# K cache transposed from rows of four keys, and probabilities kept in the V order, in a two-problem attention kernel

## The chip, the cores and the metric

The kernel runs on one core of a Trainium2 chip. The metric is device time in microseconds of one launch, the median of three runs.

## What is computed

Two independent attention problems, A and B, have the same shapes: a batch of 16, 144 queries, a model width of 448, 16 heads of width 256, and a cache of 512 keys and values for each head. All arrays are bf16.

```python
q = (x @ wq).reshape(B, Sq, H, Dh).transpose(0, 2, 1, 3)
scores = jnp.einsum("bhqd,bhkd->bhqk", q, k_cache) * (Dh ** -0.5)
p = _softmax(scores, axis=-1)
o = jnp.einsum("bhqk,bhkd->bhqd", p, v_cache)
return o.transpose(0, 2, 1, 3).reshape(B, Sq, H * Dh) @ wo
```

The two results are joined along the last axis. The softmax and the product with V do not depend on the order of the keys, as long as both use the same order.

## The kernel before

A unit is one head of one batch of one problem; there are 512 units, numbered U. Eight units form a super-group SG (64 of them), four units a group G.

For each unit the program does the following. `t_q` (L338) computes q transposed, 2 x 128 rows by 144 columns, in eight matmuls. `t_evac_q` writes it, scaled, to `qt_sb`. The 144 queries are then handled in two parts. The first 112 go unit by unit: `t_sa` (L471) makes the scores 112 x 512 in two matmuls of 512 columns, with the transposed K as the moving operand. `t_max` (L482) takes the row maximum, `t_exp` (L493) the exponential, `t_recip` and `t_norm` (L503, L511) the normalisation in `pa_sb`. `t_ta` (L524) transposes the 112 x 512 probabilities in four TensorE transposes, in which the probabilities are the loaded weights and the identity is the moving operand. `t_evac_pta` (L534) copies them to `pt_sb`. `t_pv` (L557) multiplies with V in eight matmuls of 144 columns. The last 32 queries of four units are stacked to 128 rows: `t_sb` (L374) computes the scores of eight units in 16 matmuls, four of them side by side in the array; `t_max_b`, `t_exp_b` (L397), `t_recip_b`, `t_norm_b` follow. Their transposition to `pbt_sb` is done by a DMA (`t_ptb_dma`, L425), or, in 18 super-groups at the start and the middle, by TensorE (`t_tb`, L437). `t_op_piece` (L595) does the output projection of 128-row chunks, two matmuls at a time, between the units.

K reaches SBUF through `t_load_k` (L306), one DMA transpose for each super-group: 8 x 512 keys by 256 (2 MB) from DRAM. The source is a matrix of 4096 rows of 512 bytes, and the destination, in `kt_sb`, has two runs of 4096 elements on each partition. The compiled transpose moves it in blocks of 16 rows by 128 columns. `kt_sb` has two slots (NK = 2), so the load of super-group n + 2 waits until the last `t_sa` of super-group n is done. V comes through `t_load_v` (L316), 1 MB for a group, where partition p holds the keys 4p to 4p + 3 in one run of 2 KB. So the transposes of P have to deliver the keys 4p + c for each c from 0 to 3. In the first part `t_ta` reads every fourth column of `pa_sb` for that (the keys lie there in natural order). In the second part `t_exp_b` writes its result in the order c, p while it reads the scores from PSUM with a step of four.

All loads, stores and DMA transposes are issued by SyncE in one order fixed beforehand (`dma_plan`, from L649). From super-group 8 on it repeats every 16 units: for two super-groups n and n + 1 there are a load of x where one is due, pb(n), k(n + 2), pb(n + 1), k(n + 3), and four loads of V. The order of the instructions on the other engines is written out in the loop from L740. `_Sched.add` derives the waits from reads and writes.

Of the kernel before, what the change touches and what calls it, by code (L numbers as in the profile page):

```python
# [5 lines left out]
BF16 = mybir.dt.bfloat16  # L6
F32 = mybir.dt.float32
AF = mybir.ActivationFunctionType
# [114 lines left out]
def bass_concat_heads__mha_block_cached__gqa_block_cached__near_ridge_kernel(  # L123
# [19 lines left out]
    Bn, SQ, D = A_x.shape  # L143
    H, SK, DH = A_k_cache.shape[1], A_k_cache.shape[2], A_k_cache.shape[3]
    assert (SQ, D, SK, DH) == (144, 448, 512, 256), (SQ, D, SK, DH)
    assert H % 4 == 0
    QA, QB = 112, 32
# [18 lines left out]
    NK, NV, NXG = 2, 5, 2  # L166
# [5 lines left out]
    NQT, NPA, NPB, NPT, NST, NSTB, NOST = 12, 14, 2, 8, 4, 2, 3  # L172
    NPBT = 1
    RS = 4
    RC = RS * 128
    OP_DELAY = 2
    assert NT % 8 == 0
# [4 lines left out]
    with contextlib.ExitStack() as es:  # L182
        def sb(name, shape, dt):
            return es.enter_context(nc.sbuf_tensor(name, shape, dt))

        def ps(name, shape, dt):
            return es.enter_context(nc.psum_tensor(name, shape, dt))

        wq_sb = sb("wq_sb", [128, 4, H * DH], BF16)
        wo_sb = sb("wo_sb", [128, NWO, D], BF16)  # L190
        ring = sb("ring", [128, NWO, RC], BF16)
        kt_sb = sb("kt_sb", [128, 2, NK * 8 * SK], BF16)
        v_sb = sb("v_sb", [128, NV, 4, 4 * DH], BF16)
        xt_sb = sb("xt_sb", [128, NXG, 4, XB * SQ], BF16)
        qt_sb = sb("qt_sb", [128, NQT, 2, SQ], BF16)
        pa_sb = sb("pa_sb", [128, NPA, SK], BF16)
        pb_sb = sb("pb_sb", [128, NPB, 2, SK], BF16)
# [6 lines left out]
        sa_ps = [ps("sa_ps%d" % i, [128, 512], F32) for i in range(2)]  # L204
        sb_ps = [ps("sb_ps%d" % i, [128, 512], F32) for i in range(2)]
# [94 lines left out]
        def t_load_k(SG):  # L300
            pr, r0 = divmod(8 * SG, NU)
            sl = SG % NK
            src = ks[pr].rearrange("b h k d -> (b h k) d")[r0 * SK:(r0 + 8) * SK, :]

            def e(q):
                return q.dma_start_transpose(kt_sb[:, :, sl * 8 * SK:(sl + 1) * 8 * SK], src).then_inc(  # L306
                    sems["kt%d" % sl], 16)
            S.add(SP, e, writes=[(("kt", sl), SG)], dma_sem="kt%d" % sl, name="k%d" % SG)

# [48 lines left out]
        def t_warm(k):  # L358
            def e(t):
                ins = None  # L360
                for _ in range(N_WARM[k]):
# [2 lines left out]
            S.add(PE, e, reads=[("ident", 0), ("warm", 0)], writes=[(("sbb", 1), ("w", k))], banks=["sb1"],  # L364
                  name="W%d" % k)

        def t_sb(SG):
            def e(t):
                ins = None
                for dc in range(2):  # L370
                    for jj in range(8):
                        U = 8 * SG + jj
                        j = jj % 4
                        ins = t.matmul(sb_ps[jj // 4][32 * j:32 * j + 32, :], lhsT=qt_sb[:, U % NQT, dc, QA:SQ],  # L374
                                       rhs=kt_sb[:, dc, (U % (8 * NK)) * SK:(U % (8 * NK) + 1) * SK], start=(dc == 0),
                                       stop=(dc == 1), tile_position=(0, 32 * j))
                return ins
            S.add(PE, e, reads=[(("qt", (8 * SG + jj) % NQT), 8 * SG + jj) for jj in range(8)] +
                  [(("kt", SG % NK), SG)],
                  writes=[(("sbb", 0), ("s", 2 * SG)), (("sbb", 1), ("s", 2 * SG + 1))], banks=["sb0", "sb1"],  # L380
                  name="SB%d" % SG)
# [10 lines left out]
        def t_exp_b(G):  # L392
            sl = G % NSTB
            psl = (G // 2) % NPB

            def e(a):
                return a.activation(pb_sb[:, psl, G % 2, :], sb_ps[G % 2][:, :].rearrange("q (p c) -> q c p", c=4), AF.Exp,  # L397
                                    bias=stat[:, NEGB + sl:NEGB + sl + 1], scale=1.0,
                                    accum_out=stat[:, RSUMB + sl:RSUMB + sl + 1])
            S.add(ACT, e, reads=[(("sbb", G % 2), ("s", G)), (("negb", sl), G)],  # L400
                  writes=[(("pb", psl, G % 2), (G, 0)), (("rsumb", sl), G)], banks=["sb%d" % (G % 2)], name="exb%d" % G)
# [60 lines left out]
        def t_sa(U):  # L462
            SG = U // 8
            ksl = SG % NK
            bank = U % 2
            ko = (U % (8 * NK)) * SK

            def e(t):
                ins = None
                for dc in range(2):  # L470
                    ins = t.matmul(sa_ps[bank][0:QA, :], lhsT=qt_sb[:, U % NQT, dc, 0:QA],  # L471
                                   rhs=kt_sb[:, dc, ko:ko + SK], start=(dc == 0), stop=(dc == 1))
                return ins
            S.add(PE, e, reads=[(("qt", U % NQT), U), (("kt", ksl), SG)], writes=[(("sap", bank), ("s", U))],
                  banks=["sa%d" % bank], name="SA%d" % U)
# [40 lines left out]
        def t_ta(U):  # L516
            psl = U % NPA
            bank = ta_bank[U]

            def e(t):  # L520
                src = pa_sb[0:QA, psl, :].rearrange("q (p c) -> q c p", c=4)
                ins = None
                for c in range(4):
                    ins = t.transpose(pta_ps[bank][:, c * 128:c * 128 + QA], src[:, c, :], ident[0:QA, 0:QA])  # L524
                return ins
            S.add(PE, e, reads=[(("pa", psl), (U, 1)), ("ident", 0)], writes=[(("sap", bank), ("t", U))],
                  banks=["sa%d" % bank], name="TA%d" % U)
# [11 lines left out]
        def ring_cols(pr, b):  # L539
            g0 = pr * RP + b * SQ  # L540
            return g0, g0 % RC

        def chunks_of_batch(pr, b):
            g0 = pr * RP + b * SQ
            return list(range(g0 // 128, (g0 + SQ - 1) // 128 + 1))
# [18 lines left out]
        def t_evac_ot(U):  # L564
            pr, b, h = unit(U)
            g0, c0 = ring_cols(pr, b)
            n1 = min(SQ, RC - c0)
            ob = U % 2

            def e(a):  # L570
                src = ot_ps[ob][:, 0:2 * SQ].rearrange("p (c q) -> p c q", c=2)
                ins = a.activation(ring[:, 2 * h:2 * h + 2, c0:c0 + n1], src[:, :, 0:n1], AF.Copy)  # L572
                if n1 < SQ:
                    ins = a.activation(ring[:, 2 * h:2 * h + 2, 0:SQ - n1], src[:, :, n1:SQ], AF.Copy)
                return ins
            S.add(ACT, e, reads=[(("otp", ob), U)], writes=[(("ring", r % RS, h), r) for r in chunks_of_batch(pr, b)],
                  banks=["ot%d" % ob], name="eot%d" % U)

        def chunk_rows(r):
            pr, rl = divmod(r, NCH)  # L580
            row0 = rl * 128
            m = min(128, Bn * SQ - row0)
            return pr, row0, m

        def t_op_piece(r, cs, bank):
            pr, row0, m = chunk_rows(r)
            col0 = (r % RS) * 128
            acc = op_ps if bank == "op" else qp_ps
# [11 lines left out]
            for hh in sorted(set(c // 2 for c in cs)):  # L600
                assert len(S.res[("ring", r % RS, hh)].writers) == nb, (r, hh, nb)
                rd.append((("ring", r % RS, hh), r))
            S.add(PE, e, reads=rd + [(("wo", wg), pr) for wg in sorted(set(c // WOG for c in cs))],
# [84 lines left out]
        for n in range(RAMP, NSG, 2):  # L688
            t = 8 * n
# [41 lines left out]
        def pop_items(bank, i, n):  # L731
            q = fifo[bank]
            r = q[0][0]
            cs = []
            while q and len(cs) < n and q[0][0] == r and q[0][2] <= i:
                cs.append(q.pop(0)[1])
            return r, cs

        i = s_min
        while True:  # L740
# [3 lines left out]
            n = max(k for k in range(-1, NSG) if k < 0 or sb_slot[k] <= i)  # L744
# [21 lines left out]
            for u in sas:  # L766
                if 8 <= u and u + 8 < NT:
                    t_q(u + 8)
                    t_evac_q(u + 8)
                if u % 8 == 0:  # L770
                    t_sb(u // 8)
                t_sa(u)
                if u < 8:
                    t_q(u + 8)
                    t_evac_q(u + 8)
                t_max(u)
                t_exp(u)
                last_sa = u
# [43 lines left out]
            for bank in ("op", "qp"):  # L822
                while fifo[bank] and fifo[bank][0][2] <= i and credit >= 1 and (bank == "qp" or i >= op_hold):
                    r, cs = pop_items(bank, i, OPP)
# [67 lines left out]
```

## Time and profile before

| | |
|---|---|
| median of three runs | 1217.22 us (1211.76 to 1221.06) |
| profiled execution | 1215.54 us |
| its span, first to last instruction | 1213.8 us |
| granted TensorE clock, mean | 0.992 |
| busy: TensorE, VectorE, ScalarE, GpSimd | 96%, 61%, 62%, 60% |
| DMA packets on SyncE's queue | 679424, 304.05 MB |

A busy time is the union of the intervals of an engine's instructions; a matmul's interval includes its way through the array, which overlaps the next one. Two matmuls that follow each other closely are therefore better read by the distance between their starts. PE is TensorE's matmul, PEld its weight load, which runs beside the matmuls.

### The profile page before, as it was taken

The numbers are of one execution on the slowest core, as the hardware profiler recorded it, in microseconds if no ns is written. First come the engines' busy times: TensorE is split into PE (matmuls) and PEld (weight loads), VectorE is DVE, ScalarE is ACT, GpSimd is POOL, SyncE is SP. The second block draws the span as 40 slices with busy tenths as digits, with TensorE's granted clock in tenths as the row PEclk, the third lists the DMA queues.
The fourth block names the chain that finished last, engine by engine and source line by source line (L and its number), as shares of the span: only waits on it lengthen the run. The fifth ranks groups of instructions, "written<-read, shape, count | busy, mean of one in ns | idle before, by whom it ended". The sixth has DMA issues, their size and how long they took to land.

```text
span 1213.8 us, 33200 instructions
## 1 busy us (share of the span) xinstructions
PE 1171.0 (96%) x13612; PEld 882.9 (73%) x13612; DVE 743.7 (61%) x2088; ACT 748.6 (62%) x2213; POOL 727.9 (60%) x774
## 2 busy tenths in 40 slices
PE   6898999999999999999899989999999999999989
PEld 3676777777777777777577767777777777777766
DVE  3676666656656666666566656666666566566661
ACT  2565666666656666666566656666666666566662
POOL 1675576666566666666465656666666665665661
PEclk9998999999999999999899999999999999999999
DMA  9999999999999999999999899999999999899971
GB/s 244 281 264 293 286 266 194 249 264 271 262 286 194 266 253 279 271 260 247 296 231 268 252 258 255 269 279 251 266 237 242 255 285 284 224 247 249 245 208 56
DMA packets 679577, 306.18 MB, mean 252 GB/s; under 512 B 597504, under 2 KB 610304, under 8 KB 679424
## 3 DMA queue, kind: packets, MB, share of 16 engines
q1 hardware_dynamic: 679424, 304.05, 104.6%
q8 instruction: 107, 1.75, 0.6%
q14 instruction: 46, 0.38, 0.1%
HBM read 148.90 MB, written 4.13 MB: 126 GB/s over the span
## 4 chain that ended last, share of the span: by engine, by line
PE 80%; DMA 12%; DVE 3%; POOL 2%; SPq 1%; issue 1%; ACT 1%; DVEq 0%
PE ot_ps L557 17%; PE qp_ps L338 17%; PE sa_ps L471 16%; PE op_ps L595 16%; PE sa_ps L524 7%; DMA kt_sb<-in_A_k_cache_dram 6%; DMA kt_sb<-in_B_k_cache_dram 6%; PE sb_ps L374 5%; POOL pa_sb L511 1%; DVE stat L482 1%; SPq L306 1%; POOL pb_sb L415 1%; PE sb_ps L437 1%; ACT pa_sb L493 1%; PE qp_ps L595 1%
## 5 line engine op out<-in xcount | busy, mean ns | idle before, releaser
L511 POOL TENSOR_TENSOR pa_sb<-pa_sb,stat 112x512 bf16<-112x512 bf16 x512 | 532.3, 1041 | 458.2 <-DVE stat L503 432.7
L493 ACT ACTIVATE pa_sb<-sa_ps,stat 112x512 bf16<-112x512 f32 x512 | 352.6, 689 | 405.8 <-DVE stat L482 403.6
L482 DVE TENSOR_REDUCE stat<-sa_ps 112x1 f32<-112x512 f32 x512 | 354.0, 691 | 335.3 <-PE sa_ps L471 330.7
L338 PEld LDWEIGHTS qp_ps<-xt_sb,wq_sb 128*128 128x128 bf16 x4048 | 284.1, 98 | 81.6 <-DMA wq_sb<-in_A_wq_dram 3.9
L557 PE MATMUL ot_ps<-pt_sb,v_sb 128*128 128x144 bf16 x4096 | 341.8, 226 | 0.0
L338 PE MATMUL qp_ps<-xt_sb,wq_sb 128*128 128x144 bf16 x4048 | 337.4, 227 | 4.6 <-DMA wq_sb<-in_A_wq_dram 4.2
L471 PE MATMUL sa_ps<-kt_sb,qt_sb 128*112 128x512 bf16 x1024 | 314.0, 388 | 6.0 <-DVE pt_sb L534 5.2
L595 PE MATMUL op_ps<-wo_sb,ring 128*128 128x448 bf16 x1120 | 275.1, 353 | 0.0
L557 PEld LDWEIGHTS ot_ps<-pt_sb,v_sb 128*128 128x128 bf16 x4096 | 269.5, 98 | 0.4
L524 PEld LDWEIGHTS sa_ps<-ident,pa_sb 112*128 112x128 bf16 x2048 | 159.9, 114 | 113.6 <-ACT pa_sb L493 38.3
L534 DVE COPY pt_sb<-sa_ps 128x448 bf16<-128x448 bf16 x512 | 191.4, 374 | 19.9 <-PE sa_ps L524 19.9
L572 ACT ACTIVATE ring<-ot_ps 128x288 bf16<-128x288 f32 (+8 forms) x512 | 191.0, 373 | 19.4 <-PE ot_ps L557 19.2
L524 PE MATMUL sa_ps<-ident,pa_sb 112*128 112x112 bf16 x2048 | 187.3, 213 | 6.1 <-ACT pa_sb L493 6.1
L351 DVE TENSOR_SCALAR qt_sb<-qp_ps 128x288 bf16<-128x288 f32 x252 | 115.2, 457 | 95.0 <-PE qp_ps L338 94.1
L415 POOL TENSOR_TENSOR pb_sb<-pb_sb,stat 128x512 bf16<-128x512 bf16 x128 | 133.3, 1041 | 0.0
L471 PEld LDWEIGHTS sa_ps<-kt_sb,qt_sb 128*112 128x112 bf16 x1024 | 96.8, 130 | 46.0 <-issue 28.4
L355 ACT ACTIVATE qt_sb<-qp_ps 128x288 bf16<-128x288 f32 x254 | 105.5, 415 | 33.2 <-PE qp_ps L338 31.6
L595 PEld LDWEIGHTS op_ps<-wo_sb,ring 128*128 128x128 bf16 x1120 | 96.0, 98 | 31.8 <-ACT ring L572 0.2
L493 ACT ACTIVATION_READ_ACCUMULATOR pa_sb<-sa_ps,stat 112x1 f32 x512 | 99.4, 194 | 0.0
L397 ACT ACTIVATE pb_sb<-sb_ps,stat 128x512 bf16<-128x512 f32 x128 | 88.6, 692 | 0.8
L387 DVE TENSOR_REDUCE stat<-sb_ps 128x1 f32<-128x512 f32 x128 | 87.2, 681 | 0.0
L374 PE MATMUL sb_ps<-kt_sb,qt_sb 128*32 128x512 bf16 x1024 | 69.2, 391 | 18.2 <-DMA kt_sb<-in_B_k_cache_dram 11.3
(33 smaller groups left out, 353.6 us busy)
## 6 DMA issues: line engine op xcount, KB each, us to landing
v_sb<-in_A_v_cache_dram SPq DMA_DIRECT2D x64, 1024.0 KB, 8.9
v_sb<-in_B_v_cache_dram SPq DMA_DIRECT2D x64, 1024.0 KB, 8.9
out_dram<-ost_sb SPq DMA_DIRECT2D x36, 112.0 KB, 9.7
wo_sb<-in_A_wo_dram SPq DMA_DIRECT2D x8, 448.0 KB, 9.5
wo_sb<-in_B_wo_dram SPq DMA_DIRECT2D x8, 448.0 KB, 5.2
wq_sb<-in_A_wq_dram SPq DMA_DIRECT2D x4, 768.0 KB, 6.0
wq_sb<-in_B_wq_dram SPq DMA_DIRECT2D x4, 768.0 KB, 9.7
pbt_sb<-pb_sb SPq DMA_TRANSPOSE x46, 4.9
```

The source lines that it names most:

```text
L338: ins = t.matmul(acc[:, dc * SQ:(dc + 1) * SQ], lhsT=wq_sb[:, kc, c0:c0 + 128], rhs=xt_sb[:, xsl, kc, xo:xo + SQ], start=(kc == 0 and dc = ...
L374: ins = t.matmul(sb_ps[jj // 4][32 * j:32 * j + 32, :], lhsT=qt_sb[:, U % NQT, dc, QA:SQ], rhs=kt_sb[:, dc, (U % (8 * NK)) * SK:(U % (8 * ...
L415: return g.tensor_tensor(pb_sb[:, psl, G % 2, :], pb_sb[:, psl, G % 2, :], stat[:, RINVB + sl:RINVB + sl + 1].to_broadcast([128, SK]), op= ...
L471: ins = t.matmul(sa_ps[bank][0:QA, :], lhsT=qt_sb[:, U % NQT, dc, 0:QA], rhs=kt_sb[:, dc, ko:ko + SK], start=(dc == 0), stop=(dc == 1))
L482: return v.tensor_reduce(stat[0:QA, NEG + sl:NEG + sl + 1], sa_ps[bank][0:QA, :], axis=AX.X, op=ALU.max, negate=True)
L493: return a.activation(pa_sb[0:QA, psl, :], sa_ps[bank][0:QA, :], AF.Exp, bias=stat[0:QA, NEG + sl:NEG + sl + 1], scale=1.0, accum_out=stat ...
L511: return g.tensor_tensor(pa_sb[0:QA, psl, :], pa_sb[0:QA, psl, :], stat[0:QA, RINV + sl:RINV + sl + 1].to_broadcast([QA, SK]), op=ALU.mult)
L524: ins = t.transpose(pta_ps[bank][:, c * 128:c * 128 + QA], src[:, c, :], ident[0:QA, 0:QA])
L534: return v.tensor_copy(pt_sb[:, sl, :, 0:QA], pta_ps[bank][:, 0:512].rearrange("p (c q) -> p c q", c=4)[:, :, 0:QA])
L557: ins = t.matmul(ot_ps[ob][:, dc * SQ:(dc + 1) * SQ], lhsT=v_sb[:, vsl, j, c * DH + dc * 128:c * DH + (dc + 1) * 128], rhs=pt_sb[:, sl, c, ...
L572: ins = a.activation(ring[:, 2 * h:2 * h + 2, c0:c0 + n1], src[:, :, 0:n1], AF.Copy)
L595: ins = t.matmul(acc[0:m, 0:D], lhsT=ring[:, c, col0:col0 + m], rhs=wo_sb[:, c, :], start=(c == first), stop=(c == last))
```

## The change

Four consecutive keys become one row of the source of K's transpose: 1024 rows of 2 KB in place of 4096 rows of 512 bytes. The 1024 columns of such a row are four keys by 256, and they give eight runs of 1024 elements on each partition of `kt_sb`. A run (k, dc) holds, for the half dc of the head width, the keys 4r + k. For a unit the scores' moving operand now consists of four pieces of 128 elements, 4 KB apart, where it was one piece of 512. The scores, and with them P, have their columns in the order k, r, which is the order of V. So `t_ta` reads 128 neighbouring columns for each transpose, and `t_exp_b` writes its result in the order in which it reads. The waits, the order of the instructions and their number on each engine, and the 512 blocks of 16 x 128 that one K transpose moves, are as before.

```diff
+    KR = 4
-        kt_sb = sb("kt_sb", [128, 2, NK * 8 * SK], BF16)
+        kt_sb = sb("kt_sb", [128, NK, KR, 2, 8 * SK // KR], BF16)
...
-                return q.dma_start_transpose(kt_sb[:, :, sl * 8 * SK:(sl + 1) * 8 * SK], src).then_inc(
+                return q.dma_start_transpose(kt_sb[:, sl].rearrange("p k d r -> p (k d) r"),
+                                             src.rearrange("(r k) d -> r (k d)", k=KR)).then_inc(
...
+        def kt_of(U, dc):
+            n = SK // KR
+            return kt_sb[:, (U // 8) % NK, :, dc, (U % 8) * n:(U % 8 + 1) * n]
...
-                        ins = t.matmul(sb_ps[jj // 4][32 * j:32 * j + 32, :], lhsT=qt_sb[:, U % NQT, dc, QA:SQ],
-                                       rhs=kt_sb[:, dc, (U % (8 * NK)) * SK:(U % (8 * NK) + 1) * SK], start=(dc == 0),
+                        ins = t.matmul(sb_ps[jj // 4][32 * j:32 * j + 32, :].rearrange("q (k r) -> q k r", k=KR), lhsT=qt_sb[:, U % NQT, dc, QA:SQ],
+                                       rhs=kt_of(U, dc), start=(dc == 0),
...
-                return a.activation(pb_sb[:, psl, G % 2, :], sb_ps[G % 2][:, :].rearrange("q (p c) -> q c p", c=4), AF.Exp,
+                return a.activation(pb_sb[:, psl, G % 2, :], sb_ps[G % 2][:, :], AF.Exp,
...
-                    ins = t.matmul(sa_ps[bank][0:QA, :], lhsT=qt_sb[:, U % NQT, dc, 0:QA],
-                                   rhs=kt_sb[:, dc, ko:ko + SK], start=(dc == 0), stop=(dc == 1))
+                    ins = t.matmul(sa_ps[bank][0:QA, :].rearrange("q (k r) -> q k r", k=KR),
+                                   lhsT=qt_sb[:, U % NQT, dc, 0:QA],
+                                   rhs=kt_of(U, dc), start=(dc == 0), stop=(dc == 1))
...
-                src = pa_sb[0:QA, psl, :].rearrange("q (p c) -> q c p", c=4)
+                src = pa_sb[0:QA, psl, :].rearrange("q (c p) -> q c p", c=4)
```

More of the change, by code (lines that the diff above doesn't have):

```diff
@@ L465, in t_sa @@
             bank = U % 2
-            ko = (U % (8 * NK)) * SK
             def e(t):
```

## The prediction

> **What bounds the kernel now.** I read the page first: the busy shares, then the slices.
>
> ```profile
> PE 1171.0 (96%) x13612; PEld 882.9 (73%) x13612; DVE 743.7 (61%) x2088; ACT 748.6 (62%) x2213; POOL 727.9 (60%) x774
> ...
> PE   6898999999999999999899989999999999999989
> ...
> DMA  9999999999999999999999899999999999899971
> ```
>
> TensorE and the DMA engines are both full from end to end; the other three are at 60% and will not decide. A full PE row need not mean matmuls at their pace, so I read the chain of waits over one unit in the middle (start, length, what):
>
> ```profile
> 608.62 0.43 PE sa_ps L471 x2
> 609.05 0.20 PE sa_ps L524 x4
> 609.25 0.50 PE ot_ps L557 x8
> 609.75 0.38 PE op_ps L595 x2
> ```
>
> These are 215 ns for 512 columns, 50 for 112, 62 for 144, 190 for 448: all on one line of 0.41 ns a column plus about 3 ns. TensorE is held by the columns it streams, not by its weight loads. Then the waits: what does TensorE still wait for?
>
> ```profile
> PE sb_ps L374 <- DMA kt_sb<-in_B_k_cache_dram: 11.3, 5, 5.3
> PE sb_ps L374 <- DMA kt_sb<-in_A_k_cache_dram: 6.5, 4, 3.2
> ```
>
> 17.9 us in nine waits, all of t_sb for K. Its margin elsewhere is small: taking the landing of each load from the start of its t_sb, 19 of the 64 loads landed at most 1.0 us early (among them 11 with 0.14 or less); from super-group 8 on these are almost all even ones, and the odd ones have 5 to 11 us. In the packet records SyncE's queue has nothing in flight for 102 us in all, 37 of them after 1100. So two things count: the columns on TensorE, and the length of K's load. The stages, by window (PE, PEld, DVE, ACT, POOL busy, clock, DMA share, GB/s):
>
> ```profile
> 730.00:737.00 7.00, 7.00 (x89) 5.13 (x87) 3.70 (x11) 3.32 (x10) 3.15 (x5) 1.00 1.06 391
> 744.00:749.00 5.00, 5.00 (x58) 3.89 (x58) 3.09 (x9) 2.58 (x8) 3.72 (x5) 1.00 1.28 290
> 675.50:677.00 1.50, 1.50 (x26) 0.82 (x24) 0.49 (x2) 1.05 (x5) 0.66 (x1) 1.00 0.99 168
> 677.50:683.00 5.50, 5.50 (x66) 4.38 (x65) 3.95 (x12) 3.28 (x12) 2.96 (x3) 1.00 1.28 290
> 703.00:704.20 1.20, 1.20 (x18) 0.92 (x18) 0.70 (x3) 0.89 (x5) 1.20 (x2) 1.00 1.32 282
> ```
>
> In order: V alone; K's transpose in full flow; the first 1.5 us of a K load; the rest of it; a load of x.
>
> **The change, part by part.** The base is the profiled execution, 1215.5 us (span 1213.8 and 1.7 around it). It lies 1.7 under the median of the three runs.
>
> *P's transposes (L524, 2,048 of them).* The rows of the line and of t_tb, whose weights are neighbouring columns already (min/median/max ns):
>
> ```profile
> L524 PEld LDWEIGHTS sa_ps<-ident,pa_sb x2048: 110/113/152, 30.9 to 1206.1; 112*128 112x128 bf16 x187
> L437 PEld LDWEIGHTS sb_ps<-ident,pb_sb x144: 95/98/100, 28.8 to 709.2; 128*128 128x128 bf16 x144
> ```
>
> The weight load should fall from 113 to 98 ns. Bounds: all of it on the path, 2,048 x 15 = 31 us; none, 0. What hides it is the matmul before. Over all 1,536 pairs of neighbouring L524 matmuls the starts lie 48 to 55 ns apart with few exceptions, 51.0 in the mean (78.3 us in all) against a median of 49, which is the pace of 112 columns. Only the excess can be weight load: 1,536 x 2 = 3 us. The step from L471 to L524 is 216 ns, the pace of the 512 columns before it, and hides the first load. I take -2 us, near the excess. If that cover went (a shorter moving operand), up to 15 ns each would show.
>
> The Trainium skill (TensorE: Matmul & The Clock Gate, "Back-to-back issue gap") says that in a stream of weight loads and matmuls the spacing is set by both, about 81 ns at 128 columns. By that rule the shorter load would count in full, and the estimate would be 1184; here t_tb, with 128 columns, steps by 56 ns and L524 by 49, so the trace disagrees.
>
> *Scores from four pieces (L471, L374, 2,048 matmuls).* The warm-up matmuls L362 already read four pieces of 128 columns. Once the clock is up their starts are 216 ns apart, as are those of L471 with one piece (216). 0 us. The pieces will be 4 KB apart and not 1 KB; no row shows that distance. Bounds: 0, and each piece stepping like a matmul of its own, 4 x 56 ns (t_tb, 128 columns) in place of 216, 8 ns for 1,024 matmuls of L471 and 256 sets of four of L374, 10 us. I take 0, the row with the same four pieces.
>
> *t_exp_b (L397, 128).* It loses the step of four in PSUM: 692 ns now, against 689 for L493, which reads neighbours. 0.4 us on ScalarE, which is 38% idle: 0.
>
> *K's transpose (L306, 64 of 2 MB).* The bytes, the 512 blocks and the packets of 256 bytes stay; the pitch between the 256-byte pieces goes from 512 bytes to 2 KB, and the walk over the columns has eight groups instead of two. Full flow is 290 GB/s, 7.2 us a load (2.097 MB), and with its start 9. Does the walk cost? By packet count the second group of the load at 674 begins at about 680, inside the window 677.5:683, which holds 290 without a dip. The x load passes four groups in 1.2 us at 282. So a change of group costs nothing to be seen. Bound above: each of the six further groups starts like a load, 168 in place of 290 GB/s for 1.5 us, that is 0.63 us each and 3.8 a load. Does the pitch cost? x has a pitch of 896 bytes, with every other piece off a 256-byte line, and runs at 282 all the same: the pace looks like that of the 256-byte packets and not of the memory. No row shows 2 KB. Bound above: the pace of a load's start all through, 168 GB/s, +5.3 us a load. Bound below: the slow start goes, -0.63 us a load. I take 0, the value of the two nearest rows. SyncE's queue, its waits and what stands behind them are unchanged; each of its engines gets the same number of packets.
>
> Sum: 1215.5 - 2 = 1213.5; at the median, 1.7 higher: **1215**.
>
> **The rivals.**
>
> *Slower: the 2 KB pitch slows K's stream.* Place: L306, then t_sb's wait. In a cycle of 16 units the even load comes behind the odd one and its V, so a load longer by s delays it by up to 2s. The margins decide: s = 0.45 us (273 GB/s instead of 290) costs, over the 16 loads with less than 0.9 us, 16 x 0.9 - 2.3 = 12 us; from there it is slower by 1%. At s = 0.8 it is 20 x 1.6 - 6.4 = 26 us: 1240. Beyond some 1.5 us the queue itself becomes the bound (1112 us of work now): half pace would give 1112 + 64 x 7.2 = 1575, the pace of the start (+5.3) 1450, and eight starts a load (+3.8) about 1355 to 1390. For it: no row has this pitch, the margins are thin. Against it: x at 896 bytes, and the missing dip at the change of group.
>
> The Trainium skill (DMA: Bandwidth & Descriptors, "Latency and other measured facts") gives 261 GB/s for a DMA transpose whose middle dimension is not contiguous. By that figure K's load would take 8.0 us, which is the 1240 above as an estimate; but the source of before has gaps between its pieces as well, and the trace shows 290.
>
> *Faster: the loads get shorter.* If the slow start (168 GB/s for 1.5 us) came from neighbouring rows meeting in the memory, the wider pitch would end it: 0.63 us a load, up to 1.3 on the even ones. The nine waits would shrink by about 1.1 each, 10 us, and the slow clock behind the long ones by 2: 1201. Faster loads than that end at the nine waits, 17.9 us and 4 of clock: 1192. For it: the start is slow from an idle queue (675.5:677) and behind another load (712.5:714, 136 GB/s) alike. Against it: the pitch is the same in the full flow behind the start, at 290 GB/s, so the pitch alone does not make the start slow.
>
> *No change at the weights.* The 113 ns could come from the 112 rows and not from the step of four. Then -2 becomes 0: 1217, the same case.
>
> **How the numbers follow.** A measurement of this kernel tells about 1%, 12 us, from no change (its three runs span 9). Same within 1%: 0.50, and its own range is 1205 to 1227. Slower: 0.32, half of it the small price (1228 to 1250), half the larger ones. Faster: 0.18, nearly all between 1192 and 1204. Leaving out the far slower cases (0.15) and the fastest end (0.03), the range is 1196 to 1248.
>
> **What would show it.** L524's weight loads near 98 ns with the steps of its matmuls at 49; L471's steps at 216; a window inside a K load at 290 GB/s with the median time to landing still near 12 us; the waits of t_sb for K near 18 us. The prediction is wrong if a full-flow window of K is away from 290, or dips appear at eight places in a load; then the waits of L374 for kt_sb carry the difference. It is also wrong if L471's matmuls step by more than 216.

## The result and the profile after

The changed kernel takes 1212.56 us in the median of 20 runs (1209.19 to 1216.94), the kernel before 1216.38 in 20 runs (1211.76 to 1224.01). The ratio is 0.9964, interval 0.9949 to 0.9980: 0.36% faster, some 4 us. The profiled execution took 1209.51 us, with a span of 1207.8.

The page of the changed kernel, the same rows as before:

```profile
PE 1167.9 (97%) x13612; PEld 875.3 (72%) x13612; DVE 743.6 (62%) x2088; ACT 747.8 (62%) x2213; POOL 727.0 (60%) x774
...
PE   6898999999999999999899999999999999999989
...
DMA  9999999999999999999999899999999999999981
```

Nothing has changed place: TensorE and the DMA engines are full, the rest is at 60%. The chain of waits over one unit (L476 was L471, L530 was L524, L563 was L557, L601 was L595):

```profile
609.58 0.43 PE sa_ps L476 x2
610.01 0.20 PE sa_ps L530 x4
610.21 0.50 PE ot_ps L563 x8
610.71 0.38 PE op_ps L601 x2
```

The same lengths to the last digit: neither the four pieces of K nor the neighbouring columns of P change TensorE's pace. The rows of P's transposes and of t_tb:

```profile
L530 PEld LDWEIGHTS sa_ps<-ident,pa_sb x2048: 95/96/152, 30.6 to 1200.1; 112*128 112x128 bf16 x187
L443 PEld LDWEIGHTS sb_ps<-ident,pb_sb x144: 95/97/100, 28.8 to 708.1; 128*128 128x128 bf16 x144
```

The weight load fell from 113 to 96 ns in the median, and the 112 rows had no part in it. In the path little came of it: the 1,536 steps between neighbouring transposes sum to 77.2 us, where they summed to 78.3. The windows of the changed kernel (the first 1.5 us of a K load, its full flow, V alone):

```profile
674.30:675.80 1.50, 1.50 (x26) 0.91 (x24) 0.60 (x2) 1.16 (x5) 0.77 (x1) 1.00 0.89 185
675.80:681.00 5.20, 5.20 (x61) 3.76 (x54) 3.20 (x9) 2.94 (x11) 2.05 (x3) 1.00 1.28 290
728.00:734.00 6.00, 6.00 (x78) 4.35 (x77) 3.54 (x9) 3.62 (x11) 2.89 (x4) 1.00 1.05 390
```

290 and 390 GB/s are what they were; the start of the load moved 185 where the one before moved 168. This is where the two traces differ. Cutting each K load's packets (the last 8,192 packets of 256 bytes before it lands) into sixteenths, the second 512 packets take 0.71 us in the median before and 0.51 after, and the full flow 0.45 in both. The first 512 went the other way, from 0.68 to 0.82, so that the first 1,024 together fell from 1.62 to 1.39 (all medians, which need not add up). SyncE is held by a K load for at least 7.56 us, where it was 7.72. The waits of t_sb (L380) for K:

```profile
PE sb_ps L380 <- DMA kt_sb<-in_B_k_cache_dram: 8.7, 4, 5.8
...
PE sb_ps L380 <- DMA kt_sb<-in_A_k_cache_dram: 5.2, 3, 3.7
```

13.9 us in seven waits, where it was 17.9 in nine. One profile cannot carry a difference of 4 us here, since equal kernels differ by that much from run to run; hence the experiments.

One of these waits costs more than its length. At super-group 38 `t_sb` waits 3.4 us in the kernel before, and behind that wait the granted clock stands at half for 3.4 us. The window there, in the kernel before:

```profile
714.40:717.60 3.20, 3.20 (x27) 1.88 (x20) 1.14 (x4) 0.42 (x1) 0.30 (x1) 0.50 1.28 290
```

In the changed kernel the wait at super-group 38 is 1.8 us long, and the window behind it is at the full clock:

```profile
711.50:714.70 3.20, 3.20 (x41) 1.94 (x30) 1.65 (x4) 1.17 (x4) 1.04 (x1) 1.00 1.28 290
```

The other profiles of the whole kernel, from the experiments below, agree. In five of the twelve this wait lasts 3.2 to 3.7 us, and each has 3.4 us at half clock behind it; in the other seven it lasts at most 2.2 us, and none has.

### The profile page after: what moved, and what is told of

Same layout as the page of the kernel before. It is cut to its first block, busy times and chain, and to the rows that moved or that the text cites. A ratio compares the mean times of both kernels' runs of the same rounds, so it can differ in the third digit from the quotient of the medians.

```text
span 1207.8 us, 33200 instructions
## 1 busy us (share of the span) xinstructions
PE 1167.9 (97%) x13612; PEld 875.3 (72%) x13612; DVE 743.6 (62%) x2088; ACT 747.8 (62%) x2213; POOL 727.0 (60%) x774
## 4 chain that ended last, share of the span: by engine, by line
PE 81%; DMA 11%; POOL 3%; DVE 3%; SPq 1%; issue 1%; ACT 0%; DVEq 0%
PE ot_ps L563 18%; PE qp_ps L340 17%; PE sa_ps L476 17%; PE op_ps L601 16%; PE sa_ps L530 7%; DMA kt_sb<-in_B_k_cache_dram 6%; PE sb_ps L380 5%; DMA kt_sb<-in_A_k_cache_dram 5%; POOL pa_sb L517 2%; DVE stat L488 1%; SPq L307 1%; POOL pb_sb L421 1%; PE qp_ps L601 1%; PE sb_ps L443 0%; DVE qt_sb L353 0%
## 5 line engine op out<-in xcount | busy, mean ns | idle before, releaser
L563 PE MATMUL ot_ps<-pt_sb,v_sb 128*128 128x144 bf16 x4096 | 341.5, 226 | 0.0
L476 PE MATMUL sa_ps<-kt_sb,qt_sb 128*112 128x512 bf16 x1024 | 312.6, 387 | 6.7 <-DVE pt_sb L540 5.2
L601 PE MATMUL op_ps<-wo_sb,ring 128*128 128x448 bf16 x1120 | 275.3, 353 | 0.0
L563 PEld LDWEIGHTS ot_ps<-pt_sb,v_sb 128*128 128x128 bf16 x4096 | 268.9, 98 | 0.4
L530 PEld LDWEIGHTS sa_ps<-ident,pa_sb 112*128 112x128 bf16 x2048 | 143.8, 97 | 119.0 <-ACT pa_sb L499 38.0
L530 PE MATMUL sa_ps<-ident,pa_sb 112*128 112x112 bf16 x2048 | 185.9, 212 | 5.7 <-ACT pa_sb L499 5.7
L476 PEld LDWEIGHTS sa_ps<-kt_sb,qt_sb 128*112 128x112 bf16 x1024 | 96.4, 130 | 46.3 <-issue 27.6
L601 PEld LDWEIGHTS op_ps<-wo_sb,ring 128*128 128x128 bf16 x1120 | 96.1, 98 | 31.9 <-issue 0.2
L403 ACT ACTIVATE pb_sb<-sb_ps,stat 128x512 bf16<-128x512 f32 x128 | 88.5, 691 | 0.8
L463 POOL COPY pt_sb<-pbt_sb 128x512 bf16<-128x512 bf16 x128 | 78.0, 610 | 10.9 <-PE ot_ps L563 10.9
```

Of the source, the lines that this page charges most:

```text
L476: ins = t.matmul(sa_ps[bank][0:QA, :].rearrange("q (k r) -> q k r", k=KR), lhsT=qt_sb[:, U % NQT, dc, 0:QA], rhs=kt_of(U, dc), start=(dc = ...
L563: ins = t.matmul(ot_ps[ob][:, dc * SQ:(dc + 1) * SQ], lhsT=v_sb[:, vsl, j, c * DH + dc * 128:c * DH + (dc + 1) * 128], rhs=pt_sb[:, sl, c, ...
L601: ins = t.matmul(acc[0:m, 0:D], lhsT=ring[:, c, col0:col0 + m], rhs=wo_sb[:, c, :], start=(c == first), stop=(c == last))
```

## The experiments

Two theories at first. A: the K loads got shorter at their start, and the gain comes from there. B: the gain comes from the shorter weight loads of P's transposes. The runs were made in three batches, each on one chip. Every ratio is against runs of the kernel before in the same batch.

### The part on P alone

```diff
-                src = pa_sb[0:QA, psl, :].rearrange("q (p c) -> q c p", c=4)
+                src = pa_sb[0:QA, psl, :].rearrange("q (c p) -> q c p", c=4)
...
-                return a.activation(pb_sb[:, psl, G % 2, :], sb_ps[G % 2][:, :].rearrange("q (p c) -> q c p", c=4), AF.Exp,
+                return a.activation(pb_sb[:, psl, G % 2, :], sb_ps[G % 2][:, :], AF.Exp,
```

> The part on P alone: K's load and the scores as before, P's transposes read neighbouring columns and the exponential of the last 32 queries writes in the order it reads. The keys of P and V then do not match, so the output is not the reference's; the work has the same size. Theory A (the gain of 4 us comes from shorter K loads, and the weights of P's transposes were hidden): 0.999, about 1 us, the weight loads of L524 at 98 ns, the waits of t_sb for K still near 18 us. Theory B (the gain comes from the weight loads): 0.9965, the whole 4 us, with the waits for K unchanged.

0.9998 (0.9979 to 1.0017), median 1217.19 against 1217.05 us. The weight loads of this run:

```profile
L524 PEld LDWEIGHTS sa_ps<-ident,pa_sb x2048: 95/96/152, 30.4 to 1206.5; 112*128 112x128 bf16 x187
```

The waits for K are 19.7 us, near the 18 expected. So the 17 ns are gone from each of 2,048 loads, 35 us in sum, and nothing of it shows in the time. The steps sum to 77.3 us: the 1 us that the trace shows is too small for this measurement. Theory B falls.

### The part on K alone

The diff of the change without the two edits above.

> The part on K alone: rows of 2 KB and eight runs, scores from four pieces, but P's transposes read every fourth column and the exponential writes with a step, as before. The keys of P and V do not match, so the output is not the reference's; the work has the same size. Theory A (shorter K loads): 0.9973, 3 us, weight loads of L524 at 113 ns, waits of t_sb for K near 14 us, the shortest hold of SyncE by a K load near 7.6 us. Theory B (weight loads): 1.000, no gain.

0.9981 (0.9959 to 1.0002), median 1213.88 us. The median is 3.2 us lower, as theory A has it, and the shortest hold is 7.52 us; but the interval touches 1, and the waits for K in its profile are 21.4 us (12.3 and 9.1), more than before and not near 14 as expected. By itself this run does not decide, and it shows that the total of the waits in a single profile cannot stand against a median of runs: the profiled execution took 1215.8 us, 1.9 more than the median. Of the 21.4 us, 8.5 lie in the first eight super-groups and 6.7 at the change from A to B; the other 6.2 are less than the 6.9 that the kernel before has in that place.

### Rows of two and of eight keys

```diff
-    KR = 4
+    KR = 2
```

> The changed kernel with rows of two keys (1 KB, four runs, four groups of columns). P's transposes still read neighbouring columns, so the keys of P and V do not match and the output is not the reference's. If the start of a K load gets shorter with the pitch, or with the number of groups, it lies between before and after: the second 512 packets of a load take between 0.77 and 0.50 us, and the ratio is 0.997 to 0.999. If any pitch over 512 bytes does it, it is the same as the changed kernel, 0.9964.

0.9965 (0.9944 to 0.9986). The second 512 packets take 0.55 us in the median, but the first 1,024 take 1.61, hardly less than the 1.62 of before.

```diff
-    KR = 4
+    KR = 8
```

> The changed kernel with rows of eight keys (4 KB, sixteen runs of 512, sixteen groups of columns; the scores read eight pieces of 64). P's transposes still read neighbouring columns, so the keys of P and V do not match and the output is not the reference's. If the start of a load gets shorter with the pitch, it is at most 2 us faster than the changed kernel (0.995). If a wider pitch costs the stream, windows of a load in full flow fall below 290 GB/s and it is slower than before. If pieces of 64 columns cost TensorE, the steps of L471's matmuls rise over 216 ns: each nanosecond is 1 us.

0.9965 (0.9947 to 0.9982). The full flow is 1.81 us for 2,048 packets, 290 GB/s, as before; the second 512 packets take 0.52 us; the two matmuls of the scores (L476 here) step by 216 ns also with pieces of 64 columns. So rows of 1, 2 and 4 KB gave the same time, within intervals of 0.2% each way. Since these three also share a new layout of kt_sb, a third theory had to be tried. C: it is the place of the runs in SBUF.

### The new layout with rows of one key, and the new rows in the old layout

```diff
-    KR = 4
+    KR = 1
```

> The changed kernel with rows of one key: the source of K's transpose is 4096 rows of 512 bytes as before, two runs, the scores' operand in one piece; what stays of the change in K is that each slot of kt_sb is one block of 16 KB on a partition (before, the two runs lay 16 KB apart). P's transposes read neighbouring columns, so the keys of P and V do not match and the output is not the reference's. Theory A (rows of more than one key make a load shorter): 0.9995, the first 1024 packets of a load 1.65 us in the mean as before. Theory C (the place of the runs in SBUF does it, since rows of 1, 2 and 4 KB gave the same): 0.9965.

0.9996 (0.9978 to 1.0015), and the second 512 packets take 0.66 us, near the 0.71 of before. With the layout, the neighbouring columns and rows of 512 bytes nothing is gained.

```diff
-        kt_sb = sb("kt_sb", [128, NK, KR, 2, 8 * SK // KR], BF16)
+        kt_sb = sb("kt_sb", [128, KR, 2, NK * 8 * SK // KR], BF16)
...
-                return q.dma_start_transpose(kt_sb[:, sl].rearrange("p k d r -> p (k d) r"),
+                return q.dma_start_transpose(kt_sb[:, :, :, sl * 8 * SK // KR:(sl + 1) * 8 * SK // KR].rearrange("p k d r -> p (k d) r"),
...
-            return kt_sb[:, (U // 8) % NK, :, dc, (U % 8) * n:(U % 8 + 1) * n]
+            return kt_sb[:, :, dc, (U % (8 * NK)) * n:(U % (8 * NK) + 1) * n]
```

> The changed kernel with rows of four keys, but the eight runs of a slot lie 4 KB apart, the other slot's runs between them; the output is the reference's. Theory A (rows): 0.9965, as the changed kernel. Theory C (each slot one block): 1.000, as before.

0.9977 (0.9955 to 0.9999), median 4.0 us lower, second 512 packets 0.54 us. It lies on the side of theory A, though its interval only just leaves 1. With the run before it, theory C falls.

### The changed kernel again

> The changed kernel once more, for a second profile. Theory A: 0.9965, the first 1024 packets of a load again near 1.53 us in the mean and the shortest hold of SyncE near 7.56 us; the waits of t_sb for K, 13.9 us in the first profile of it, may move by 5 us, since the one profile of the part on K alone had 21 us.

0.9970 (0.9951 to 0.9989): the gain comes again. The profile is less tidy. The shortest hold is 7.61 us and the second 512 packets take 0.58 us; but the first 1,024 packets take 1.69 us in the mean, not 1.53. That expectation missed, and by that measure the start was no shorter than before (1.65). It may be that the mean over a start also holds what the load waits for behind V; that was not tested. The waits for K are 18.3 us (10.9 and 7.4).

The length of a whole load separates the kernels better than its start. With the packets counted off in the order of the queue, a load takes from its first packet to its last 8.86 to 8.95 us in the mean in the four profiles of the whole kernel with rows of 512 bytes, and 8.68 to 8.84 in the eight with wider rows. That is 0.12 us less, from 8.89 to 8.77.

### The loads by themselves

> The loads by themselves: no attention is computed and the output is zeros. 64 loads of K from rows of 512 bytes (two runs of 4096, each slot one block), each waiting only for the load before last; the first 32 back to back, the last 32 with two loads of V (1 MB each) between. If wider rows shorten a load by itself, the 32 back to back take 0.1 to 0.2 us more for each than in the run with rows of 2 KB, with the second 512 packets of a load near 0.7 us in the median; the span is 5 to 12 us longer. If the difference needs the kernel around it, both take the same to 0.3%.

> The same loads from rows of 2 KB, eight runs; no attention is computed and the output is zeros. If wider rows shorten a load by itself, the second 512 packets take 0.5 us in the median and the full flow is at 290 GB/s in both.

743.96 us against 732.83 in the median of two runs each, which lie within 2 us of each other. The spans are 741.6 and 730.0, 11.6 us or 0.18 for each of the 64 loads. From the landings, the loads back to back come every 8.24 and 7.97 us, those with two loads of V between every 14.24 and 14.15. First SyncE's rows with 512-byte rows:

```profile
L307 SPq DMA_TRANSPOSE kt_sb<-in_A_k_cache_dram x32: 7849/8172/8602, 18.9 to 274.3; - x32
```

and with 2 KB rows:

```profile
L307 SPq DMA_TRANSPOSE kt_sb<-in_A_k_cache_dram x32: 7618/7889/8300, 18.9 to 265.6; - x32
```

The hold (min/median/max ns) is 0.28 us shorter in the median. The bytes moved tell the same. The windows of the loads back to back, with 512-byte rows (DVE and POOL busy, clock, DMA share, GB/s):

```profile
60.00:140.00 80.00, 0.00 (x0) 0.00 (x0) 1.00 1.19 254
```

and with 2 KB rows:

```profile
60.00:140.00 80.00, 0.00 (x0) 0.00 (x0) 1.00 1.18 262
```

All sixteenths in the middle of a load take 0.45 us in both, so the difference lies where one load meets the next: 8.24 - 16 x 0.45 leaves about 1.0 us a load there, and 0.8 with the wide rows. Counted in the order of the queue, the first 512 packets of a load back to back take 1.24 us in the median with 512-byte rows and 0.99 with 2 KB rows; the other sixteenths agree within 0.04. Two forecasts missed: the slow part did not sit in the second 512 packets here, and the difference back to back was 0.27 us a load and not 0.1 to 0.2. Wider rows do shorten a load by itself, and no other engine has a part in it.

### What the shorter loads are worth: one V load moved

The margins of before named a place: even K loads came with 1.7 us to spare in the mean from super-group 10 on (14 of 27 with at most 1.0 us), odd ones with 7.4. The four V loads of a cycle stand behind the odd load, and so ahead of the next even one. One of them was moved in front of the odd load, behind the even one.

```diff
-            for j, at in enumerate((5, 5, 5, 8)):
+            for j, at in enumerate((-2, 5, 5, 8)):
```

> The changed kernel with one of the four V loads of a cycle of 16 units issued between the two K loads (right behind the even one) instead of behind the odd one. If the rest of the loss on TensorE is the even loads' margin (0 to 3 us before t_sb starts, against 5 to 11 of the odd ones), each even load comes up to 2.7 us earlier and each odd one as much later: the waits of t_sb for K from super-group 10 on fall from some 10 us to under 3, ratio 0.989 to 0.993. If V's earlier place only moves the queue's work, 0.9965.

0.9898 (0.9876 to 0.9920), median 1205.95 us, the fastest version so far. The even loads now come with 3.7 us to spare in the mean. The waits for K from super-group 10 on are one wait of 4.2 us at the change from A to B, more than the 3 expected in all, and none elsewhere. The same edit was then made in the kernel before, and the changed kernel with it was run again beside it:

> The kernel before (rows of 512 bytes, P every fourth column) with one V load issued between the two K loads, as in the fastest run so far. If shorter loads count only through the even loads' margin, then with that margin widened they count for little: this one lies within 0.2% of the same with rows of four keys, near 0.990. If they count through the work of the queue as a whole, it is 0.3% to 0.4% behind it, near 0.9935.

> The changed kernel with one V load between the two K loads once more, on the same chip as the run before: 0.9898 again, waits of t_sb for K near 11 us, of which over half at the start and at the change from A to B.

Both give 0.9885 (0.9854 to 0.9916, and 0.9857 to 0.9912), medians 1205.89 and 1205.34 us. First the waits for K of the kernel before with this edit, whose even loads now have 3.4 us to spare in the mean (4 of 27 with at most 1.0):

```profile
PE sb_ps L374 <- DMA kt_sb<-in_A_k_cache_dram: 6.8, 3, 3.5
...
PE sb_ps L374 <- DMA kt_sb<-in_B_k_cache_dram: 3.1, 1, 3.1
```

and those of the changed kernel with it:

```profile
PE sb_ps L380 <- DMA kt_sb<-in_A_k_cache_dram: 6.4, 4, 3.1
...
PE sb_ps L380 <- DMA kt_sb<-in_B_k_cache_dram: 4.0, 2, 3.0
```

About 10 us in each, most of it in the ramp and at the change from A to B. Once the even loads have their margin, the whole change in K and P is worth 0.5 us, where six runs of one kernel spread over 2 to 3; a 95% interval worked out from the six runs of each reaches from about -1 to +2 us, clear of the 4 that it is worth without the edit. The shorter loads count through the even loads' margin, and hardly otherwise.

The profiles show the same path. Take the waits of `t_sb` for K over 0.2 us from super-group 10 on, and leave out the one at the change from A to B. They sum to 6.9, 7.3 and 8.1 us in the three profiles with rows of 512 bytes and V in its old place, to 2.9 to 6.2 in the six with wider rows, and to 0, 0 and 1.0 in the three with the V load moved. The spans of these executions are 1213.8 to 1216.0, 1207.8 to 1214.0 and 1205.1 to 1206.1 us, and over the twelve they rise with these waits (correlation 0.98). The mean margin of the even loads, however, did not grow in the changed kernel (1.74 and 1.69 us in its two profiles, 1.73 before): a TensorE that waits less also comes sooner to the next `t_sb`. That reading of the margin is an argument and was not tested.

## Why the prediction was right, and which step was not

The time, 1212.6, lies in the range and in the case called likeliest, within 1%. The forecast of 2 us off the profiled execution has the right sign, and the kernel gained 3.8 in the medians of 20 runs. But the sum got its gain from the wrong term: the 2 us were to come from P's transposes, which gave nothing that a run can show, and the gain came from K's transpose, which was put at 0. That the sum is so near the result is luck.

*P's transposes.* The weight load fell as forecast (98 forecast, 96 ns measured), and the cover named, the matmul before it, holds: the steps fell by 1.1 us and not by the 2 taken, and the run on this part alone shows nothing at all (0.9998). Nothing near the bound of 31 us came. The rule of the Trainium skill (TensorE: Matmul & The Clock Gate, "Back-to-back issue gap") that weight load and matmul both set the spacing does not bind in this kernel: 17 ns less load left the step of 49 ns where it was.

*Scores from four pieces; the exponential.* 216 ns a step, with four pieces and with eight, and 691 ns for L403 against 692. Both were taken at 0, and are 0.

*K's transpose.* Half right. The full flow stayed at 290 GB/s with pitches of 512 bytes, 1, 2 and 4 KB, and eight groups of columns bring no dips. So the slower rival did not come. The figure of 261 GB/s of the Trainium skill (DMA: Bandwidth & Descriptors, "Latency and other measured facts") is not the pace of the full flow, but it is near that of whole loads back to back, their starts included (254 and 262 GB/s in the windows of the loads by themselves). The prediction set that figure against the full flow alone, and so read a whole load of 8.0 us as a slower one; the kernel before took 8.9. The step that failed is "I take 0, the value of the two nearest rows": both rows are of the full flow, and the change acts where a load begins. The bound below named that place, -0.63 us a load, and the rival built on it was given 0.18. Measured by itself it is -0.18 us (0.27 back to back, 0.09 behind V), and -0.12 in the kernel. The start stays slow, only less so. What the prediction held against that rival, that the full flow has the same pitch and is not slow, did not exclude it. Through the even loads' margin the shorter loads give nearly all of the 4 us, in proportion about what the rival's own reckoning makes of it: 0.63 us was to give 12, and 0.18 gives some 3.5.

Why a load from wide rows begins sooner stays open. Pitch, number of column groups, number of rows and the length of the runs in `kt_sb` change together in KR, and no run here took them apart.

## What to carry to other kernels

A weight load that is hidden behind the matmul before it is worth its exposed part, and that part is read from the starts of the matmuls, not from the length of the loads: 35 us of it vanished here without a trace in the time. When a stream's steady pace is settled, price its beginning too: between 0.1 and 0.2 us less at each of 64 starts was nearly the whole effect. And where two kinds of loads alternate, compare their margins first: moving one V load from behind the slack load, where it held up the tight one, to behind the tight one brought the kernel before 1.15%, three times what the change itself brought, and took its worth away.

## What the runs showed that was not expected

In the kernel before, a K load in full flow stops for more than a microsecond now and then. The window behind such a point:

```profile
742.00:743.00 1.00, 1.00 (x18) 0.96 (x17) 1.00 (x4) 1.00 (x4) 0.11 (x1) 1.00 0.12 5
```

5 GB/s, in the middle of a load. An instruction packet (16 KB on queue q8, of which the page counts 107) starts at 741.5 and takes 1.1 us. Over all 64 loads, the 10 in whose time no such packet falls take 8.1 us from their first packet to the last, the other 54 take 9.1. In the two runs of the loads by themselves there is no packet on q8, and none of the sixteenths between a load's second and its last takes 0.8 us; in the kernel before 27 of them take over 1.0, and in 22 of these such a packet is on its way. The two coincide. The runs of the loads alone lack all other work as well, so whether the one makes the other was not tested.
